# Another division of the first batch, units by quarters of w_out, half-head tile pairs and a load in four parts in a fused attention and feed-forward kernel

## The chip, the core and the metric

The kernel runs on one core of a Trainium2 chip. A core has engines that run side by side, each with its own in-order list of instructions: TensorE (PE, matrix products; its weight loads are shown as PEld), VectorE (DVE), ScalarE (ACT), GpSimd (POOL) and SyncE (SP), which here issues nearly all DMA transfers. They wait for each other through semaphores. Matrix products land in PSUM, a small memory that VectorE and ScalarE read; everything else lies in SBUF. The metric is device time in microseconds (us); lower is better.

## What is computed

A linear attention with cosine weights, then a feed-forward layer on its output:

```python
def phi(x, c, s):
    r = np.maximum(x, 0.0)
    return np.concatenate([r * c, r * s], axis=-1)
q_p = phi(q, cos_w, sin_w)          # q, k, v: 8 batches, 8 heads, 576 rows, 64 wide
k_p = phi(k, cos_w, sin_w)
kv = np.einsum('bhsf,bhsd->bhfd', k_p, v)
z = np.sum(k_p, axis=2)
num = np.einsum('bhsf,bhfd->bhsd', q_p, kv)
den = np.einsum('bhsf,bhf->bhs', q_p, z)[..., None] + 1e-06
x = (num / den)                     # then transposed to 4608 rows of 512
h = x @ w_in                        # 512 x 2048
g = np.maximum(0.01 * h, h)
out = g @ w_out                     # 2048 x 512
```

cos_w and sin_w depend on the row alone.

## The kernel before

**Tiling.** Rows are worked in nine groups of 512: for each of the eight batches its first 512 rows (four tiles of 128, `J = 4`), and a ninth group of the 64 rows left over in each batch. All products take 16-bit operands. A group goes through these steps:

- loads of q, k and v (`load_main`, and `load_kvtail` for the 64 leftover rows) into float32 buffers of the pool `stage` (seven of them, shared with the weights);
- `q_prep`, `k_main` and `k_tail` make relu(x)·cos and relu(x)·sin in 16 bits; the arithmetic of all three is in the helper `phi_half` (L220 when ScalarE does it, L222 on another engine). `v_main` and `v_tail` cast v (helper `copy`, L228 on ScalarE, L230 elsewhere);
- the prepared q is transposed, on TensorE (`q_transpose`, L329, with a copy out of PSUM into `qpT`) for the first two batches and by DMA (L310) after that;
- `kv_mm` (L260, L270) forms k·v with its column of ones for z, four heads at a time; the result is copied to `kv` (L291 for a half of the heads, L282 for all);
- `num` (L339) or, for a pair of tiles on half the heads, `num_half` (L374) multiplies qpT with kv; `divide` (L350, L354, L355, all on VectorE) makes the quotient;
- the quotient is transposed into xT: `x_transpose_half` (L391, copy L395), `x_transpose` (L403) or a DMA (L321);
- `ffn1` (L417) is product one, in 16 column tiles m of w_in, each of four chunks of depth; ScalarE applies the leaky relu to two tiles at once (L425);
- `ffn2` (L440) is product two, in units (tile, quarter): a quarter is four of the 16 depth tiles and needs one of four loads of w_out. After the fourth quarter of a tile the result is copied (`ffn2_out`) and written out (L454).

**Order.** The order of the instructions on every engine is the order in which the program writes them. For the first two batches (numbered 0 and 1 in the code) it is written out by hand; from then on `weave` puts steps (`at(position, step)`) between units of products one and two by their positions. An engine that waits holds up everything behind it in its list.

**PSUM.** There are three pools of buffers: `h` and `o` with two buffers each, `n` with one. A step that takes a buffer waits until the previous user's reader is done.

**Loads.** All loads are issued by SyncE and share one hardware queue; at most eight transfers are tracked at a time, so the ninth is issued when the first has landed. The order at the start is: q in two halves of the heads, the tails of k and v, k and v in halves of the heads, w_in in eight pieces (`load_w1`, L138; cast by POOL in `cast_w1`), two quarters of w_out (`load_w2`, L142; cast by VectorE in `cast_w2`), q of batch 1 and its tails, the other two quarters, k and v of batch 1 in halves, and then q, k and v of batch 2 (the third batch).

**Dummy products.** `idle(n)` (L162) puts n products of zeros into TensorE's list where it would otherwise stand still.

**The stretch that the change touches.** For batch 0 VectorE prepares all of q, the k tail, the v tail and most of k; ScalarE copies the four qpT, casts half of v and does two pieces of k. Product one of batch 0 begins on half-width tiles as soon as a pair of row tiles is ready. In batch 1's part, the units of product two of batch 0 run in this order, with four q transposes of batch 1 between them:

```python
order = [(0, 0), (1, 0), (2, 0), (3, 0), (0, 1), (1, 1), (2, 1), (3, 1), (2, 2), (3, 2)]
```

and the rest of its units lie between the k·v products and numerators of batch 1.

Of the kernel before, what the change touches and what calls it, by code (L numbers as in the profile page):

```python
# [9 lines left out]
dt = mybir.dt  # L10
# [8 lines left out]
def kernel(  # L19
# [61 lines left out]
    def load_main(nm, src, b, parts=(0, 1)):  # L81

        if parts[0] == 0:
            st[nm, b] = stage.tile([P, H, J, D], dt.float32, name=f"{nm}st", tag="stage")
        lo, hi = 4 * parts[0], 4 * parts[-1] + 4
        nc.sync.dma_start(  # L86
            st[nm, b][:, lo:hi],
            src[b, lo:hi, 0:MAIN, :].rearrange("h (p j) d -> p h j d", j=J),
        )
# [26 lines left out]
    def load_halves(b):  # L116
# [5 lines left out]
    w1 = [  # L122
        [const.tile([P, 2, 512], dt.float16, name=f"w1_{i}_{cp}") for cp in range(2)]
        for i in range(DFF // 512)
    ]
# [7 lines left out]
    def load_w1(i, cp):  # L133

        if cp == 0:
            st["w1", i] = stage.tile([P, NKC, 512], dt.float32, name="w1st", tag="stage")
        sl = slice(2 * cp, 2 * cp + 2)
        nc.sync.dma_start(st["w1", i][:, sl], w1v[:, sl, 512 * i : 512 * (i + 1)])  # L138
# [11 lines left out]
    for i in range(NB):  # L150
        for cp in range(2):
            load_w1(i, cp)
# [73 lines left out]
    def copy(eng, o, i):  # L226
        if eng is ACT:
            nc.scalar.copy(o, i)  # L228
        else:
            eng.tensor_copy(o, i)  # L230
# [69 lines left out]
    def q_prep(g, j, lo=0, hi=H):  # L300
        src, c, _ = q_src(g, j)
        if lo == 0:
            st["qp", g, j] = qppool.tile([P, H, F], dt.float16, name="qp", tag="qp")
        qp = st["qp", g, j]
        phi_half(DVE, qp[:, lo:hi, 0:D], src[:, lo:hi], cos_t[:, c : c + 1])
        phi_half(DVE, qp[:, lo:hi, D:F], src[:, lo:hi], sin_t[:, c : c + 1])
# [59 lines left out]
    def num_half(g, jp, hg, where):  # L366

        if hg == 0:
            st["xp", g, jp] = qppool.tile([P, 2, H, D], dt.float16, name="xp", tag="qp")
        ps = psum(where, [P, 2, 512], dt.float32, "ps_numh")  # L370
        for o in range(2):
            for hh in range(4):
                h = 4 * hg + hh
                nc.tensor.matmul(  # L374
                    ps[:, o, hh * NE : (hh + 1) * NE],
                    lhsT=st["qpT", g, 2 * jp + o][:, h, :],
                    rhs=kv[g][:, h, :],
                )
        divide(ps, st["xp", g, jp][:, :, 4 * hg : 4 * hg + 4, :])

    def x_transpose_half(g, jp, hg, ps=None, out=True):

        if ("xT", g) not in st:
            st["xT", g] = xtpool.tile([P, NKC, MAIN], dt.float16, name="xT")
        xp = st["xp", g, jp]
        if ps is None:
            ps = psum("o", [P, 2, 2 * P], dt.float16, "ps_xth")
        for cc in range(2):
            for o in range(2):
                h = 4 * hg + 2 * cc  # L390
                nc.tensor.transpose(  # L391
                    ps[:, cc, o * P : (o + 1) * P], xp[:, o, h : h + 2, :], ident
                )
        if out:
            nc.scalar.copy(  # L395
                st["xT", g][:, 2 * hg : 2 * hg + 2, jp * 2 * P : (jp + 1) * 2 * P], ps
            )
# [10 lines left out]
    def ffn1(g, m, lo=0, hi=MAIN, chunks=range(NKC), where="h"):  # L408
# [7 lines left out]
        for c in chunks:  # L416
            nc.tensor.matmul(  # L417
                ps[:, m % 2, lo:hi],
                lhsT=w1[m // 4][c // 2][:, c % 2, m % 4 : 512 : 4],
                rhs=xT[:, c, lo:hi],  # L420
                start=(c == 0 and lo == 0),
                stop=(c == NKC - 1 and hi == MAIN),
            )
# [61 lines left out]
    def cast_w1(i, cp, eng):  # L485
        sl = slice(2 * cp, 2 * cp + 2)
        copy(eng, w1[i][cp], st["w1", i][:, sl])

    def cast_w2(i, eng):
        copy(eng, w2[:, 4 * i : 4 * i + 4, :], st["w2", i])  # L490
# [3 lines left out]
    for hg in range(2):  # L494
        for j in range(2):
            q_prep(0, j, 4 * hg, 4 * hg + 4)
    for j in range(J):
        if j > 1:
            q_prep(0, j)
        q_transpose(0, j, ACT)  # L500
        idle(1)
    kp_tiles(0)
    k_tail(0, DVE, DVE)
    v_tail(0, DVE)
    for j in range(J):
        k_main(0, j, DVE, DVE, 0, 4)
    v_main(0, 0, 4, ACT)
    for j in range(2):
        k_main(0, j, ACT, DVE, 4, 8)
    idle(6)  # L510
    kv_half(0, 0, "o")
    for j in range(2, J):
        k_main(0, j, DVE, DVE, 4, 8)
    v_main(0, 4, 6, DVE)
    v_main(0, 6, 8, ACT)
    idle(1)
    num_half(0, 0, 0, "n")
    num_half(0, 1, 0, "h")
    idle(3)
    kv_half(0, 1, "o")  # L520
    for i in range(NB):
        for cp in range(2):
            cast_w1(i, cp, POOL)
    x_transpose_half(0, 0, 0)
    num_half(0, 0, 1, "n")
    half = 2 * P
    for m in range(2):
        ffn1(0, m, 0, half, range(0, 2))
    x_transpose_half(0, 1, 0)
    for m in range(2, 4):  # L530
        ffn1(0, m, 0, half, range(0, 2))
    num_half(0, 1, 1, "n")
    x_transpose_half(0, 0, 1)
    for m in range(4):
        ffn1(0, m, half, MAIN, range(0, 2))
# [14 lines left out]
    load_main("q", q, 2)  # L550
# [37 lines left out]
    cast_w2(3, DVE)  # L588
# [4 lines left out]
    for j in range(J):  # L593
        at(5 + j, q_transpose, 1, j, ACT, "h")
        at(9, k_main, 1, j, ACT, DVE, 0, 4)
    at(9, v_main, 1, 0, 2, DVE)
    at(9, v_main, 1, 2, 4, ACT)
    order = [(0, 0), (1, 0), (2, 0), (3, 0), (0, 1), (1, 1), (2, 1), (3, 1), (2, 2), (3, 2)]
    weave([(n, f2(0, 4 * tt + part)) for n, (tt, part) in enumerate(order)], steps)
    for tt in (2, 3):  # L600
        ffn2(0, 4 * tt + 3, None)
    ffn2_out(0, 2, DVE)
    ffn2_out(0, 3, DVE)
    ffn2(0, 2)
    kv_half(1, 0, "h", False)
    k_main(1, 0, ACT, DVE, 4, 8)
    kv_half_out(1, 0)
    for j in range(1, J):
        k_main(1, j, ACT if j < 3 else DVE, DVE, 4, 8)
    v_main(1, 4, 6, POOL)  # L610
    v_main(1, 6, 8, ACT)
    ffn2(0, 4 + 2)
    num_half(1, 0, 0, "h")
    num_half(1, 1, 0, "n")
    ffn2(0, 3, None)
    kv_half(1, 1, "h")
    ffn2_out(0, 0, ACT)
    ffn2_mm(0, 1, 12, 14)
    num_half(1, 0, 1, "h")
    num_half(1, 1, 1, "h")  # L620
    ps = psum("n", [P, 2, MAIN], dt.float16, "ps_x")
    for jp in range(2):
        x_transpose_half(1, jp, 0, ps[:, :, jp * 2 * P : (jp + 1) * 2 * P], False)
    nc.scalar.copy(st["xT", 1][:, 0:2, :], ps)  # L624
    ffn2_mm(0, 1, 14, 16)
    ffn2_out(0, 1, DVE)
    ps = psum("o", [P, 2, 2, 2 * P], dt.float16, "ps_x1")
    x_transpose_half(1, 0, 1, ps[:, 0])
    for m in range(2):
        ffn1(1, m, 0, MAIN, range(0, 2))  # L630
    x_transpose_half(1, 1, 1, ps[:, 1])
    for m in range(2, 4):
        ffn1(1, m, 0, MAIN, range(0, 2))
    for m in range(4):
        ffn1(1, m, 0, MAIN, range(2, 4))
# [4 lines left out]
    for m in range(4, NFT):  # L640
        units.append((8 + m / 2, f1(1, m, "n" if m < 6 else "h")))
# [39 lines left out]
    kv_steps(2, 9.7, 0.5, 13, DVE, 2)  # L681
    for j in range(J):
        at(13.5 + 1.1 * j, num, 2, j)
        at(14.8 + 1.1 * j, x_transpose, 2, j, "o" if j < 2 else "h")
# [53 lines left out]
```

## Time and profile before

| | |
|---|---|
| median of 3 runs | 295.77 us (295.47 to 295.80) |
| profiled execution | 296.48 us |
| its span, first to last instruction | 294.7 us |
| TensorE clock granted over the span | 1.00 |
| HBM read, written | 36.70 MB, 9.44 MB |
| product one (L417) | 592 matmuls, 142.6 us busy |
| product two (L440) | 560 matmuls, 139.5 us busy |
| dummy products (L162) | 28 |

The span and everything in the profile come from one execution, whose time is 0.7 us above the median. In the lists of groups and in the timeline an instruction is named by line, engine, operation and what it writes and reads; `x8` is a count; in brackets stands how long the engine had been idle and who released it. A matmul's recorded length overlaps that of the next, so the distance of starts, and not the length, tells how long one holds TensorE. Busy shares in tenths over 40 slices of 7.4 us show where the engines work:

```
PE   7799999999999999999999999999999999999995
DVE  6951488945846816823562356233323211000011
ACT  4846366754352722642263226322222232222200
DMA  7999999999999999989683997416671211011132
```

The DMA engines are busy without a break for the first 17 slices (to about 125 us), most densely to 60 us.

### The profile page before, as it was taken

What the parts mean: (1) busy time and instruction counts of PE and PEld (TensorE: products, weight loads), DVE (VectorE), ACT (ScalarE), POOL (GpSimd) and SP (SyncE); (2) the same over time, 40 slices, a digit from 0 to 9 for tenths busy, and PEclk for the clock granted to TensorE, in tenths of its full rate; (3) what the DMA queues carried; (4) which work ended last, traced back from release to release, by engine and by line L of the source; (5) the groups of instructions that cost most, each with busy time, mean ns of one, the idle gap of its engine ahead of it and who ended that gap; (6) DMA issues with size and microseconds to landing.
All of it is one profiled execution on the core that took longest, in us unless ns stands there. A gap on an engine that the chain in (4) does not pass through costs nothing.

```text
span 294.7 us, 4802 instructions
## 1 busy us (share of the span) xinstructions
PE 286.4 (97%) x1932; PEld 153.9 (52%) x1932; DVE 129.9 (44%) x329; ACT 117.9 (40%) x143; POOL 11.0 (4%) x20
## 2 busy tenths in 40 slices
PE   7799999999999999999999999999999999999995
PEld 3585556565465455555545554555445544444444
DVE  6951488945846816823562356233323211000011
ACT  4846366754352722642263226322222232222200
POOL 2064000000000000000000000000000000000000
PEclk9999999999999999999999999999999999999999
DMA  7999999999999999989683997416671211011132
GB/s 222 361 385 406 325 362 331 300 155 336 232 271 325 179 265 335 178 158 332 171 152 82 292 276 148 107 55 145 145 160 51 73 53 38 36 46 60 39 71 71
DMA packets 88773, 56.93 MB, mean 193 GB/s; under 512 B 56880, under 2 KB 81712, under 8 KB 88240
## 3 DMA queue, kind: packets, MB, share of 16 engines
q1 hardware_dynamic: 88672, 56.57, 74.2%
q8 instruction: 15, 0.25, 0.4%
q14 instruction: 6, 0.05, 0.1%
q10 hardware_dynamic: 80, 0.07, 0.1%
HBM read 36.70 MB, written 9.44 MB: 157 GB/s over the span
## 4 chain that ended last, share of the span: by engine, by line
PE 81%; DMA 8%; SPq 6%; ACT 1%; issue 1%; DVE 1%; ACTq 0%
PE ps_h L417 38%; PE ps_o L440 37%; SPq L96 4%; DMA w2st<-in_moe_w_out_dram 4%; DMA w1st<-in_moe_w_in_dram 4%; PE ps_num L339 3%; PE ps_kv L270 2%; SPq L86 1%; DMA out_dram<-osb 1%; SPq L138 1%; ACT vmain L228 1%; SPq L142 1%; PE ps_kv L260 1%; DVE w L230 0%; PE ps_numh L374 0%
## 5 line engine op out<-in xcount | busy, mean ns | idle before, releaser
L417 PE MATMUL ps_h<-xT,w 128*128 128x512 f16 (+1 forms) x592 | 142.6, 373 | 0.3 <-ACT xT L624 0.2
L440 PE MATMUL ps_o<-w,g 128*128 128x512 f16 x560 | 139.5, 379 | 0.3 <-DVE w L230 0.3
L425 ACT ACTIVATE g<-ps_h 128x1024 f16<-128x1024 f32 x72 | 73.5, 1024 | 132.9 <-PE ps_h L417 132.7
L417 PEld LDWEIGHTS <-w 128*128 128x128 f16 x592 | 64.4, 113 | 52.3 <-issue 0.3
L440 PEld LDWEIGHTS <-g 128*128 128x128 f16 x560 | 54.1, 98 | 62.0 <-issue 0.6
L230 DVE COPY osb<-ps_o 128x512 f32<-128x512 f32 x34 | 23.4, 690 | 80.1 <-PE ps_o L440 80.1
L350 DVE TENSOR_SCALAR den<-ps_num 128x8 f32<-128x8 f32 x28 | 4.6, 166 | 52.9 <-PE ps_num L339 52.9
L355 DVE TENSOR_TENSOR xs<-ps_num,rden 128x512 f16<-128x512 f32 x28 | 19.4, 691 | 1.0
L222 DVE TENSOR_SCALAR qp<-qst,cos_t 128x512 f16<-128x512 f32 (+1 forms) x34 | 15.8, 465 | 4.9 <-DMA qst<-in_q_dram 4.9
L222 DVE TENSOR_SCALAR kpm<-kst,sin_t 128x512 f16<-128x512 f32 (+1 forms) x40 | 16.5, 428 | 0.8 <-DMA kst<-in_k_dram 0.8
L222 DVE TENSOR_SCALAR qp<-qst,sin_t 128x512 f16<-128x512 f32 (+1 forms) x34 | 15.8, 465 | 0.0
L339 PEld LDWEIGHTS <-qpT 128*128 128x128 f16 (+1 forms) x256 | 11.2, 101 | 7.3 <-issue 1.7
L222 DVE TENSOR_SCALAR kpm<-kst,cos_t 128x512 f16<-128x512 f32 (+1 forms) x29 | 13.0, 449 | 0.1
L228 ACT CAST vmain<-vst 128x1024 f16<-128x1024 f32 (+1 forms) x14 | 12.9, 953 | 0.4 <-DMA vst<-in_v_dram 0.3
L339 PE MATMUL ps_num<-kv,qpT 128*128 128x66 f16 (+1 forms) x256 | 12.4, 194 | 0.0
L270 PEld LDWEIGHTS <-kpm 128*128 128x128 f16 x256 | 10.5, 97 | 2.6 <-DVE kpm L222 0.7
L228 ACT COPY qpT<-ps_qt 128x1024 f16<-128x1024 f16 x8 | 7.8, 1019 | 7.0 <-PE ps_qt L329 7.0
L162 PE MATMUL ps_idle<-blank 128*128 128x512 f16 x28 | 9.1, 462 | 1.2 <-DVE blank L157 1.2
L230 DVE CAST w<-w2st 128x2048 f16<-128x2048 f32 x4 | 4.9, 1228 | 10.7 <-DMA w2st<-in_moe_w_out_dram 10.7
L230 POOL CAST w<-w1st 128x1024 f16<-128x1024 f32 x8 | 8.3, 1042 | 15.1 <-DMA w1st<-in_moe_w_in_dram 15.0
L270 PE MATMUL ps_kv<-vmain,kpm 128*128 128x66 f16 x192 | 8.1, 193 | 0.0
L354 DVE RECIPROCAL rden<-den 128x8 f32<-128x8 f32 x36 | 7.3, 203 | 1.2
(57 smaller groups left out, 97.1 us busy)
## 6 DMA issues: line engine op xcount, KB each, us to landing
out_dram<-osb SPq DMA_DIRECT2D x32, 256.0 KB, 2.5
qst<-in_q_dram SPq DMA_DIRECT2D x7, 1024.0 KB, 6.5
kst<-in_k_dram SPq DMA_DIRECT2D x6, 1024.0 KB, 8.8
vst<-in_v_dram SPq DMA_DIRECT2D x6, 1024.0 KB, 8.9
w1st<-in_moe_w_in_dram SPq DMA_DIRECT2D x8, 512.0 KB, 11.0
w2st<-in_moe_w_out_dram SPq DMA_DIRECT2D x4, 1024.0 KB, 11.5
kst<-in_k_dram SPq DMA_DIRECT2D x4, 512.0 KB, 8.7
vst<-in_v_dram SPq DMA_DIRECT2D x4, 512.0 KB, 8.7
```

Of the source, the lines that this page charges most:

```text
L96: nc.sync.dma_start(t[o * TAIL : (o + 1) * TAIL], v4[o])
L162: nc.tensor.matmul(ps, lhsT=blank[:, 0:P], rhs=blank)
L222: eng.tensor_scalar(out=o, in0=i, scalar1=0.0, scalar2=col, op0=ALU.max, op1=ALU.mult)
L228: nc.scalar.copy(o, i)
L230: eng.tensor_copy(o, i)
L270: nc.tensor.matmul(ps[:, (2 * cc + o) * NE : (2 * cc + o + 1) * NE], lhsT=kpm[:, h, j, :], rhs=vmain[b % 2][:, h, j, :], start=False, stop ...
L339: nc.tensor.matmul(ps[lo:hi, h // 4, (h % 4) * NE : (h % 4 + 1) * NE], lhsT=qpT[:, h, lo:hi], rhs=kv[b][:, h, :],)
L354: nc.vector.reciprocal(rden, den)
L355: nc.vector.tensor_tensor(out=xs, in0=ps[:, :, 0 : 4 * NE].rearrange("p a (b e) -> p a b e", e=NE)[:, :, :, 0:D], in1=rden.rearrange("p (a ...
L417: nc.tensor.matmul(ps[:, m % 2, lo:hi], lhsT=w1[m // 4][c // 2][:, c % 2, m % 4 : 512 : 4], rhs=xT[:, c, lo:hi], start=(c == 0 and lo == 0 ...
L425: nc.scalar.activation(st["g", g][:, m - 1 : m + 1, :], ps, AF.Lrelu)
L440: nc.tensor.matmul(st["ps_o", g, tt], lhsT=st["g", g][:, m, tt * P : (tt + 1) * P], rhs=w2[:, m, :], start=(m == 0), stop=(m == NFT - 1),)
```

## The change

What it does:

- Batch 0: ScalarE prepares the fourth tile of q and takes the cos half of k more often; POOL casts the v tail and a quarter of v; VectorE copies one of the four qpT. The transposes of q and the dummy products (32 instead of 28) stand in another order. The first piece of w_in is loaded and cast in two. Both numerators of the second half of the heads are formed one behind the other, in different PSUM buffers.
- Product two of batch 0: the units run quarter by quarter over all four tiles, up to the third quarter; two more units stand ahead of the first k·v product of batch 1, and none are left after the second. The q transposes of batch 1 stand one unit later. The cast of the last quarter of w_out is in two halves.
- Batch 1: the transposes of the first half of the heads go through two `o` buffers and two copies, instead of one `n` buffer and one copy; ScalarE copies out two of the four results of product two instead of one. Product one of batch 1 takes its first six column tiles in two halves of the depth, instead of four tiles.
- Batch 2: q is loaded in four loads by partitions (56, 40, 24, 8). Its k·v product, numerators and transposes stand one position later.

```diff
+    def load_main(nm, src, b, parts=(0, 1), span=(0, P)):
...
-            st[nm, b][:, lo:hi],
-            src[b, lo:hi, 0:MAIN, :].rearrange("h (p j) d -> p h j d", j=J),
+            st[nm, b][p0:p1, lo:hi],
+            src[b, lo:hi, J * p0 : J * p1, :].rearrange("h (p j) d -> p h j d", j=J),
...
-    for i in range(NB):
-        for cp in range(2):
-            load_w1(i, cp)
+    w1_parts = [(0, 0, 1), (0, 1, 1), (0, 2, 2)]
+    for i in range(1, NB):
+        w1_parts += [(i, 0, 2), (i, 2, 2)]
+    for part in w1_parts:
+        load_w1(*part)
...
+    def x_transpose_half_out(g, jp, hg):
+        nc.scalar.copy(
+            st["xT", g][:, 2 * hg : 2 * hg + 2, jp * 2 * P : (jp + 1) * 2 * P],
+            st["xth", g, jp, hg],
+        )
...
     for hg in range(2):
-        for j in range(2):
-            q_prep(0, j, 4 * hg, 4 * hg + 4)
+        for j in range(J):
+            q_prep(0, j, 4 * hg, 4 * hg + 4, ACT if j == 3 else DVE)
+    kp_tiles(0)
+    q_transpose(0, 0, ACT)
+    idle(1)
+    q_transpose(0, 1, ACT)
+    idle(1)
+    k_tail(0, DVE, DVE)
+    v_tail(0, POOL)
+    k_main(0, 0, ACT, DVE, 0, 4)
+    for j in range(1, J):
+        k_main(0, j, DVE, DVE, 0, 4)
+    q_transpose(0, 2, ACT, "n")
+    idle(1)
+    v_main(0, 0, 2, DVE)
+    v_main(0, 2, 4, ACT)
+    q_transpose(0, 3, DVE)
+    idle(9)
+    kv_half(0, 0, "o")
     for j in range(J):
-        if j > 1:
-            q_prep(0, j)
-        q_transpose(0, j, ACT)
-        idle(1)
-    kp_tiles(0)
-    k_tail(0, DVE, DVE)
-    v_tail(0, DVE)
-    for j in range(J):
-        k_main(0, j, DVE, DVE, 0, 4)
-    v_main(0, 0, 4, ACT)
-    for j in range(2):
         k_main(0, j, ACT, DVE, 4, 8)
+    num_half(0, 0, 0, "h")
+    num_half(0, 1, 0, "n")
+    v_main(0, 4, 6, ACT)
+    v_main(0, 6, 8, POOL)
     idle(6)
-    kv_half(0, 0, "o")
-    for j in range(2, J):
-        k_main(0, j, DVE, DVE, 4, 8)
-    v_main(0, 4, 6, DVE)
-    v_main(0, 6, 8, ACT)
-    idle(1)
-    num_half(0, 0, 0, "n")
-    num_half(0, 1, 0, "h")
-    idle(3)
+    x_transpose_half(0, 0, 0)
     kv_half(0, 1, "o")
...
+    ps = psum("h", [P, 2, 512], dt.float32, "ps_numh")
     for m in range(2):
-        ffn1(0, m, 0, half, range(0, 2))
-    x_transpose_half(0, 1, 0)
+        ffn1(0, m, 0, half, range(0, 1))
+    num_half(0, 0, 1, None, ps)
+    num_half(0, 1, 1, "n")
+    for m in range(2):
+        ffn1(0, m, 0, half, range(1, 2))
+    for m in range(2):
+        ffn1(0, m, half, MAIN, range(0, 2))
+    x_transpose_half(0, 0, 1)
...
-    load_main("q", q, 2)
+    for p0, p1 in ((0, 56), (56, 96), (96, 120), (120, P)):
+        load_main("q", q, 2, span=(p0, p1))
...
-    cast_w2(3, DVE)
+    cast_w2(3, DVE, 0, 2)
+    cast_w2(3, DVE, 2, 4)
...
-        at(5 + j, q_transpose, 1, j, ACT, "h")
-        at(9, k_main, 1, j, ACT, DVE, 0, 4)
-    at(9, v_main, 1, 0, 2, DVE)
-    at(9, v_main, 1, 2, 4, ACT)
-    order = [(0, 0), (1, 0), (2, 0), (3, 0), (0, 1), (1, 1), (2, 1), (3, 1), (2, 2), (3, 2)]
+        at(6 + j, q_transpose, 1, j, ACT, "h")
+    order = [(tt, part) for part in range(3) for tt in range(J)]
...
     for tt in (2, 3):
         ffn2(0, 4 * tt + 3, None)
     ffn2_out(0, 2, DVE)
     ffn2_out(0, 3, DVE)
-    ffn2(0, 2)
     kv_half(1, 0, "h", False)
     k_main(1, 0, ACT, DVE, 4, 8)
     kv_half_out(1, 0)
+    ffn2(0, 3, None)
...
-    ffn2(0, 4 + 2)
+    ffn2_out(0, 0, ACT)
     num_half(1, 0, 0, "h")
     num_half(1, 1, 0, "n")
-    ffn2(0, 3, None)
+    ffn2(0, 7, None)
     kv_half(1, 1, "h")
-    ffn2_out(0, 0, ACT)
-    ffn2_mm(0, 1, 12, 14)
+    ffn2_out(0, 1, ACT)
+    x_transpose_half(1, 0, 0)
+    x_transpose_half(1, 1, 0)
     num_half(1, 0, 1, "h")
-    num_half(1, 1, 1, "h")
-    ps = psum("n", [P, 2, MAIN], dt.float16, "ps_x")
-    for jp in range(2):
-        x_transpose_half(1, jp, 0, ps[:, :, jp * 2 * P : (jp + 1) * 2 * P], False)
-    nc.scalar.copy(st["xT", 1][:, 0:2, :], ps)
-    ffn2_mm(0, 1, 14, 16)
-    ffn2_out(0, 1, DVE)
-    ps = psum("o", [P, 2, 2, 2 * P], dt.float16, "ps_x1")
-    x_transpose_half(1, 0, 1, ps[:, 0])
+    num_half(1, 1, 1, "n")
     for m in range(2):
         ffn1(1, m, 0, MAIN, range(0, 2))
-    x_transpose_half(1, 1, 1, ps[:, 1])
+    x_transpose_half(1, 0, 1)
     for m in range(2, 4):
         ffn1(1, m, 0, MAIN, range(0, 2))
-    for m in range(4):
+    x_transpose_half(1, 1, 1)
+    for m in range(4, 6):
+        ffn1(1, m, 0, MAIN, range(0, 2), "n")
+    for m in range(6):
         ffn1(1, m, 0, MAIN, range(2, 4))
...
-    for m in range(4, NFT):
-        units.append((8 + m / 2, f1(1, m, "n" if m < 6 else "h")))
+    for m in range(6, NFT):
+        units.append((8 + m / 2, f1(1, m)))
...
-    kv_steps(2, 9.7, 0.5, 13, DVE, 2)
+    kv_steps(2, 9.7, 0.5, 14, DVE, 2)
     for j in range(J):
-        at(13.5 + 1.1 * j, num, 2, j)
-        at(14.8 + 1.1 * j, x_transpose, 2, j, "o" if j < 2 else "h")
+        at(14.5 + 1.1 * j, num, 2, j)
+        at(15.8 + 1.1 * j, x_transpose, 2, j, "o" if j < 2 else "h")
```

## Prediction

> **What bounds the kernel now.** I read the page's busy shares first, then TensorE's waits, then the timeline of the first 62 us, then the issues and landings of the loads.
>
> ```profile
> span 294.7 us, 4802 instructions
> ...
> PE 286.4 (97%) x1932; PEld 153.9 (52%) x1932; DVE 129.9 (44%) x329; ACT 117.9 (40%) x143; POOL 11.0 (4%) x20
> ```
>
> TensorE is the bound; what can be won is its idle time. The list of its waits (total us, times, longest) is short:
>
> ```profile
> PE ps_numh L374 <- ACT kv L291: 1.1, 2, 0.9
> ...
> PE ps_o L440 <- DVE w L230: 0.3, 1, 0.3
> ...
> PE ps_h L417 <- ACT xT L624: 0.2, 1, 0.2
> ```
>
> Warm matmuls of 512 columns start 0.216 us apart (the 52 of the last stretch of the chain take 11.24), transposes 0.056, 66-column ones 0.032, 256-column ones 0.109. Against these pitches TensorE is gap-free from 53 us on, but for 0.6 us at 102 us, in code that the diff does not touch. So the change can act in two places: the front, and 40 to 53 us. The front (start, length, engine; in brackets the idle time before):
>
> ```profile
> 15.91 0.38 ACT L291 CAST kv<-ps_kvh 128x264 f16<-128x264 f32 x1 [1.15 <-PE ps_kvh L270]
> ...
> 16.80 0.17 DVE L350 TENSOR_SCALAR den<-ps_numh 128x8 f32<-128x8 f32 x1
> ...
> 17.98 0.43 PE L374 MATMUL ps_numh<-kv,qpT 128*128 128x66 f16 x8
> ...
> 18.45 0.17 DVE L350 TENSOR_SCALAR den<-ps_numh 128x8 f32<-128x8 f32 x1 [0.52 <-PE ps_numh L374]
> ...
> 19.64 0.40 PE L391 MATMUL ps_xth<-ident,xp 128*128 128x128 f16 x4
> ...
> 19.87 12.27 PE L417 MATMUL ps_h<-xT,w 128*128 128x256 f16 x64
> ```
>
> The second numerator (17.98) waits until the first's division has freed the one "n" buffer; its division starts 0.52 us idle; the last transposes start at 19.64. From there TensorE runs without a gap until 42.4. Then:
>
> ```profile
> 39.00 1.23 DVE L230 CAST w<-w2st 128x2048 f16<-128x2048 f32 x1 [0.78 <-DMA w2st<-in_moe_w_out_dram]
> ...
> 40.67 1.89 PE L440 MATMUL ps_o<-w,g 128*128 128x512 f16 x8
> ...
> 42.90 2.75 PE L440 MATMUL ps_o<-w,g 128*128 128x512 f16 x12 [0.34 <-DVE w L230]
> ...
> 47.67 0.62 POOL L230 CAST vmain<-vst 128x512 f16<-128x512 f32 x1 [21.40 <-DMA vst<-in_v_dram]
> ...
> 49.54 0.59 ACT L228 COPY osb<-ps_o 128x512 f32<-128x512 f32 x1
> ...
> 51.91 1.02 PE L417 MATMUL ps_h<-xT,w 128*128 128x512 f16 x4 [0.18 <-ACT xT L624]
> ```
>
> The third quarter of w_out lands just before 39.00 and is ready at 40.23; TensorE takes it up at 40.67, only 0.44 later. The fourth makes TensorE wait at 42.40 (40.67 + 8 x 0.216) until 42.90. Three more gaps follow by the pitches: 0.20 (before 49.69), 0.25 (before 51.33), 0.34 (before 51.91). Together 1.29 us.
>
> **The change, part by part.**
>
> *First batch.* VectorE keeps 12 of 16 q halves: starts 0.263 apart (rows 4.63, 4.90, 5.17), six from 4.63, six from 6.22, done 7.80 (before: 8.80). The k tail takes two, to 8.33. k's first half lands at 8.87 (issue 4.57 + 4.3); seven pieces to 10.7, v's piece 0.42 to 11.1. ScalarE has four q pieces (0.41 each, pace of L220) from 4.97, done 7.0, before the first qpT copy (7.3, unchanged). The first product k.v starts at 11.15 instead of 12.02, its copy at 11.95 instead of 13.53 (ScalarE is free), the first two numerators at 12.35 instead of 13.94. VectorE's copy of qpT 3 out of PSUM is not in this trace: at least 0.69 (128x512 out of PSUM, row L355), at most twice that; it ends at 12.5 at the latest, before k's second half lands (12.65), so it costs nothing.
> VectorE then does four k pieces and no v: free at 13.71 instead of 14.57. Divisions (1.04 apart, 1.13 long) end at 14.83 and 15.86. ScalarE, though, now does four k pieces from 12.71 and v (0.62): ready 14.97, so the second k.v product starts at 15.11 (before 15.09), its copy ends at 16.32 (before 16.29). Nothing won to here. The two numerators now have a buffer each: 16.42 and 16.68, divisions back to back from 16.87, end 18.0 and 19.03, last transposes 19.15. Front gain 19.64 - 19.15 = 0.49 us. The first w1 piece, halved, lands at about 14.8 (half of 1.36 before 15.5) and is cast by 15.5: hidden.
>
> *Units by quarters.* Product two now starts at 31.98 - 0.49 = 31.49. Eight units (4 x 0.216 = 0.865) and three transposes of q (8 x 0.056 = 0.445; the fourth has moved behind the ninth unit) bring TensorE to the third quarter at 31.49 + 6.92 + 1.34 = 39.75. It is ready at 40.23 + 0.05 whatever TensorE does, since no load ahead of it changes in bytes or order. TensorE waits 0.53: the front's gain is gone here. From 40.28 there are no waits: six units, one transposed q, k.v, numerators and two more units until the second k.v at 40.28 + 8 x 0.865 + 0.445 + 0.63 + 0.51 = 48.79. The fourth quarter (first half cast by 42.25) is needed at 44.2: its 0.50 stall is gone. k.v ends at 49.42, where before it ended at 49.2 with 4 matmuls (0.86) still to do.
>
> *Pairs on half the heads.* Now ScalarE's order counts: kv copy 49.61, osb copy 49.89 to 50.48 (0.28 behind it, as 49.26 and 49.54 before). The second transposes need the "o" buffer that this osb copy frees: 50.53, a new wait of 0.9. Then numerators, xT copy 50.96 to 51.55, and product one of batch 2 at 51.60 instead of 51.91. Its first 24 matmuls with two transposes end at 51.60 + 5.19 + 0.45 = 57.24; before 51.91 + 5.19 + 0.22 = 57.32. Sum so far: -0.08 us.
>
> *POOL beside VectorE.* In the changed order VectorE's k pieces run from 46.75 to 48.1, so the 0.62 us cast of v on POOL (47.67) falls on them; before they ended at 47.56. What that does is shown once:
>
> ```profile
> 1.69 0.62 DVE L205 CAST vmain<-ones 128x64 f16<-128x64 f32 x1
> 1.72 1.06 POOL L208 MEMSET vtail<- 128x528 f16 x2
> ...
> 3.00 0.20 DVE L205 CAST vmain<-ones 128x64 f16<-128x64 f32 x1
> ```
>
> The same cast takes 0.62 beside a POOL memset and 0.20 without. If VectorE is held until POOL ends (48.29), its last k piece frees it at 48.57 instead of 48.05, the divisions end at 50.74 and the second transposes start at 50.80 instead of 50.53: +0.27. Bounds: 0 and +0.4; I take +0.27, by the row. [...] The POOL cast of the v tail at 7.1 can hold VectorE by some 0.6 likewise; 0.5 of it falls into the wait for k at 8.3 to 8.87.
>
> *q in four loads, k.v of batch 3 one position later.* q, k and v of that batch land at 50.7, 53.8 and 57.4 (issue plus time to landing). VectorE prepares them from 53.3 on, about 61.2 done; k.v now comes after 24 more matmuls, at 62.45 (before: 60.77, with VectorE done at 60.82). Cover 1.2 us, cost nothing. Four more dummy matmuls lie in waits.
>
> Sum: -0.49 (front) + 0.53 (third quarter) - 0.50 (fourth) - 0.79 (three old gaps) + 0.89 (second transposes) + 0.34 (wait for xT, 51.26 to 51.60) + 0.27 (POOL) = +0.25 us; by the end times above -0.08 + 0.27 = +0.19. The 0.06 between them is rounding in the pitches; I take +0.2. The profiled run took 296.48 (span 294.7, 1.8 around it); the median is 295.77. On the median: 295.95 us.
>
> **Rivals.**
> *The gain gets through (faster).* If the third quarter lands 0.5 us earlier, its wait is gone and, with POOL the one that waits, the sum is -0.6: 295.2. For it: all loads run in one backlogged queue (w_out's quarters land 10.1 to 13.4 us after issue), and small shifts add up. Against: nothing ahead of it is smaller. Chance 0.18.
> *The third quarter later (slower).* Each 0.1 us later costs 0.1 in the new order; before, 0.44 were free. Landing at 39.5 instead of 39.0 gives +0.7: 296.5. It decides as soon as the landing slips. Against: the three runs lie within 0.33 us. Chance 0.15.
> *q's four loads delay k and v (slower).* If 56, 40, 24 and 8 partitions use fewer DMA engines, at half the rate q takes 6 us instead of 3, v lands at 60.4, VectorE needs 2.7 more (58.10 to 60.82 before): 63.1 against 62.45, +0.65 and so 296.6. It decides from a landing of v after 59.75. The trace has no load of such a shape. Chance 0.1. [...]
> *It does not do what it says*: the front is not faster. Up to 0.5 us of that costs nothing either, since the third quarter waits anyway; this belongs to the forecast.
>
> **Numbers.** Forecast, gains and new waits cancel, 295.95: 0.52, own range 295.4 to 296.4. Faster rival 0.18, the two slower ones 0.25, unnamed 0.05 (shared). Range for 8 in 10: 295.0 to 296.8, from the faster case to just past the slower ones. Faster by over 0.2% (0.6 us, what a measurement can tell): 0.2; within: 0.52; slower: 0.28.
>
> **What would show it.** Last front transposes near 19.15; a TensorE wait on VectorE's w cast of some 0.5 us near 39.75 and none at 42; a wait on ScalarE's osb or VectorE's xp of 0.9 to 1.2 near 49.7; product one of batch 2 at 51.6 to 51.9; a k piece beside POOL stretched near 47.7; no wait at k.v of batch 3. It is wrong if the third quarter lands elsewhere than near 39.0, or if a gap opens after 57 us.

## The result, and the profile after

| | before | changed kernel |
|---|---|---|
| median, runs side by side (6 each) | 295.78 us (295.47 to 296.32) | 298.64 us (297.48 to 300.37) |
| a second set | 295.69 us (17 runs) | 298.13 us (296.78 to 299.60, 6 runs) |
| ratio, first set | | 1.0105, 95% interval 1.007 to 1.014 |
| ratio, second set | | 1.0084, 95% interval 1.0053 to 1.0115 |
| span of the profiled execution | 294.7 us | 297.2 us, in the second set 295.5 us |

The changed kernel is about 1% slower; 295.95 us had been predicted. It also varies: its twelve runs lie over 3.6 us, the 23 of before over 1 us (in the later sets before, too, has single runs up to 298.6). So two profiled executions of it are read here, the first of 298.95 us and one from the second set of 297.32 us. The first one's page, with the row of the clock granted to TensorE in tenths over 40 slices:

```profile
span 297.2 us, 4829 instructions
...
PE 287.9 (97%) x1936; PEld 154.8 (52%) x1936; DVE 128.5 (43%) x325; ACT 120.0 (40%) x151; POOL 12.7 (4%) x24
...
PEclk9979999999999999999999999999999999999999
```

TensorE is still the bound, and the clock is not full in the third slice (14.9 to 22.3 us). From its list of TensorE's waits (total us, times, longest), where before had kv, w and xT:

```profile
PE ps_kvh L277 <- DVE vmain L237: 1.4, 1, 1.4
PE ps_xth L398 <- DVE xp L362: 1.2, 3, 0.6
...
PE ps_numh L382 <- ACT kv L298: 0.5, 1, 0.5
...
PE ps_h L429 <- ACT xT L406: 0.2, 1, 0.2
```

No wait on w (the quarters of w_out) is left, neither the new one that was predicted for the third nor the old one for the fourth. In the same execution's timeline (start, length, engine, and in brackets the idle time before):

```profile
10.49 0.35 DVE L229 TENSOR_SCALAR kpm<-kst,sin_t 128x256 f16<-128x256 f32 x1 [1.66 <-DMA kst<-in_k_dram]
...
12.80 0.41 PE L277 MATMUL ps_kvh<-vmain,kpm 128*128 128x66 f16 x8 [1.38 <-DVE vmain L237]
...
14.50 2.56 PE L169 MATMUL ps_idle<-blank 128*128 128x512 f16 x6
...
21.65 0.39 PE L398 MATMUL ps_xth<-ident,xp 128*128 128x128 f16 x4
...
52.79 0.40 PE L398 MATMUL ps_xth<-ident,xp 128*128 128x128 f16 x4 [0.64 <-DVE xp L362]
...
53.86 0.81 PE L429 MATMUL ps_h<-xT,w 128*128 128x512 f16 x3 [0.16 <-ACT xT L406]
```

Here k's first half came 1.6 us late (work on it at 10.49, 8.87 predicted), the six dummy products took 2.56 us because the clock had halved (0.50 from 14.70 to 18.12 us; the second execution shows them with 1.46), the front's last transposes began at 21.65 instead of 19.64, and product one of the second batch at 53.86 instead of 51.91. In the second profiled execution none of that is there, and the front is the predicted one to 0.04 us: work on k at 8.86, the first k·v at 11.13, its copy at 11.95, numerators at 12.38, the second k·v at 15.09, the last transposes at 19.11. VectorE begins the cast of w_out's third quarter at 38.01, TensorE comes to that quarter at 39.69 and does not wait there. The loss comes later:

```profile
38.01 1.23 DVE L237 CAST w<-w2st 128x2048 f16<-128x2048 f32 x1 [0.70 <-DMA w2st<-in_moe_w_out_dram]
...
39.69 1.03 PE L452 MATMUL ps_o<-w,g 128*128 128x512 f16 x4
...
60.66 1.29 DVE L237 CAST vmain<-vst 128x1024 f16<-128x1024 f32 x2 [0.46 <-DMA vst<-in_v_dram]
61.87 0.60 DVE L237 CAST vtail<-vtl 64x256 f16<-64x256 f32 x2
62.50 0.49 DVE L229 TENSOR_SCALAR kpm<-kst,cos_t 128x512 f16<-128x512 f32 x1
...
62.90 0.48 DVE L229 TENSOR_SCALAR kpm<-kst,sin_t 128x512 f16<-128x512 f32 x1
...
63.44 0.33 PE L277 MATMUL ps_kv<-vmain,kpm 128*128 128x66 f16 x5 [0.59 <-DVE kpm L229]
```

v of the third batch has only landed at 60.6 us (57.38 in before). VectorE waits for it, does the last pieces of k behind it, and TensorE stands in the middle of the third batch's k·v. Why v is late shows in the traffic of the DMA engines. The windows of the first profiled execution (stretch, its length, busy time of PE, PEld, DVE, ACT and POOL, clock, busy share of the DMA engines, GB/s; the share adds up the times of packets, which overlap, so it can pass 1):

```profile
42.00:46.00 4.00, 4.00 (x32) 2.23 (x29) 2.05 (x6) 3.35 (x7) 0.00 (x0) 1.00 1.11 301
46.00:50.00 4.00, 4.00 (x49) 2.42 (x48) 1.94 (x5) 2.65 (x8) 0.61 (x1) 1.00 1.12 199
50.00:54.00 4.00, 2.95 (x48) 2.12 (x46) 3.05 (x12) 2.80 (x6) 0.00 (x0) 1.00 1.11 161
```

and the same of the kernel before:

```profile
42.00:46.00 4.00, 3.66 (x30) 1.85 (x29) 3.36 (x8) 2.21 (x5) 0.00 (x0) 1.00 1.10 348
46.00:50.00 4.00, 3.96 (x63) 2.59 (x60) 3.50 (x12) 2.85 (x7) 0.62 (x1) 1.00 1.10 347
50.00:54.00 4.00, 3.73 (x39) 2.27 (x36) 3.72 (x10) 2.22 (x4) 0.00 (x0) 1.00 1.12 303
```

From 46 us on the DMA engines are as busy (1.11 and 1.12, before 1.10 and 1.12) and move little more than half. The second execution has 297, 211 and 214 GB/s in the same stretches. A packet of 1 KB takes 52 ns on average in before between 46 and 50 us, 92 and 87 ns in the two executions of the changed kernel.

### The profile page after: what moved, and what is told of

It is laid out like the page before. It is cut to its first block, busy times and chain, and to the rows that moved or that the text cites. A ratio compares the mean times of both kernels' runs of the same rounds, so it can differ in the third digit from the quotient of the medians.

```text
span 297.2 us, 4829 instructions
## 1 busy us (share of the span) xinstructions
PE 287.9 (97%) x1936; PEld 154.8 (52%) x1936; DVE 128.5 (43%) x325; ACT 120.0 (40%) x151; POOL 12.7 (4%) x24
## 4 chain that ended last, share of the span: by engine, by line
PE 90%; DVE 3%; DMA 3%; ACT 1%; SPq 1%; issue 1%; ACTq 0%
PE ps_h L429 42%; PE ps_o L452 39%; PE ps_num L346 3%; PE ps_kv L277 2%; DMA kst<-in_k_dram 2%; DVE kpm L229 1%; SPq L97 1%; PE ps_idle L169 1%; DMA out_dram<-osb 1%; PE ps_xth L398 1%; DVE xp L362 1%; ACT vmain L235 1%; DVE osb L237 1%; PE ps_qt L336 1%; PE ps_kv L267 1%
## 5 line engine op out<-in xcount | busy, mean ns | idle before, releaser
L237 DVE COPY osb<-ps_o 128x512 f32<-128x512 f32 x33 | 22.7, 691 | 81.0 <-PE ps_o L452 79.6
L362 DVE TENSOR_TENSOR xs<-ps_num,rden 128x512 f16<-128x512 f32 x28 | 19.4, 691 | 1.0
L229 DVE TENSOR_SCALAR kpm<-kst,cos_t 128x512 f16<-128x512 f32 (+1 forms) x26 | 11.9, 458 | 0.0
L169 PE MATMUL ps_idle<-blank 128*128 128x512 f16 x32 | 10.6, 480 | 1.2 <-DVE blank L164 1.2
L235 ACT COPY qpT<-ps_qt 128x1024 f16<-128x1024 f16 x7 | 7.0, 1010 | 5.8 <-PE ps_qt L336 5.8
L237 DVE CAST w<-w2st 128x2048 f16<-128x2048 f32 (+1 forms) x5 | 5.0, 1013 | 9.1 <-DMA w2st<-in_moe_w_out_dram 9.1
L237 POOL CAST w<-w1st 128x1024 f16<-128x1024 f32 (+1 forms) x9 | 8.5, 946 | 2.6 <-DMA w1st<-in_moe_w_in_dram 2.6
```

Source lines behind the costliest of these rows:

```text
L169: nc.tensor.matmul(ps, lhsT=blank[:, 0:P], rhs=blank)
L229: eng.tensor_scalar(out=o, in0=i, scalar1=0.0, scalar2=col, op0=ALU.max, op1=ALU.mult)
L362: nc.vector.tensor_tensor(out=xs, in0=ps[:, :, 0 : 4 * NE].rearrange("p a (b e) -> p a b e", e=NE)[:, :, :, 0:D], in1=rden.rearrange("p (a ...
```

## The experiments

Twelve runs were made, each beside the kernel before on the same chip. "Span" is that of the profiled execution.

| kernel | median us | ratio to before, 95% interval | span |
|---|---|---|---|
| front alone | 295.91 | 1.0008 (0.9999 to 1.0017) | 293.4 |
| q in four loads alone | 297.67 | 1.0062 (1.0044 to 1.0080) | 296.0 |
| middle alone | 297.07 | 1.0044 (1.0032 to 1.0056) | 295.1 |
| changed kernel again | 298.13 | 1.0084 (1.0053 to 1.0115) | 295.5 |
| q in four loads of 32 rows | 297.69 | 1.0067 (1.0043 to 1.0091) | 296.0 |
| q in four loads by heads | 295.81 | 0.9997 (0.9987 to 1.0008) | 294.1 |
| q in four loads of every fourth row | 296.16 | 1.0008 (0.9990 to 1.0026) | 294.0 |
| changed kernel, q in one load | 296.29 | 1.0016 (1.0005 to 1.0026) | 294.8 |
| the same, less on VectorE | 296.06 | 1.0007 (0.9996 to 1.0018) | 293.7 |
| before, fourth batch's k·v later | 295.98 | 1.0007 (0.9994 to 1.0019) | 293.8 |
| less on VectorE, fourth batch's k·v later | 296.02 | 1.0013 (1.0000 to 1.0025) | 293.6 |
| before, fifth batch's k·v later | 295.16 | 0.9981 (0.9968 to 0.9995) | 293.3 |

### One part at a time

From the first profile the front looked guilty, with 2 us lost by 22 us. So the three parts of the diff were put into the kernel before one at a time (theory 1 blames the front, theory 2 q's loads, theory 3 the middle), and the changed kernel was run once more. The front is everything of the diff up to the end of batch 0's product one; the middle everything from the cast of w_out's last quarter to `units`; q's part is

```diff
-    load_main("q", q, 2)
+    for p0, p1 in ((0, 56), (56, 96), (96, 120), (120, P)):
+        load_main("q", q, 2, span=(p0, p1))
...
-    kv_steps(2, 9.7, 0.5, 13, DVE, 2)
+    kv_steps(2, 9.7, 0.5, 14, DVE, 2)
...
-        at(13.5 + 1.1 * j, num, 2, j)
-        at(14.8 + 1.1 * j, x_transpose, 2, j, "o" if j < 2 else "h")
+        at(14.5 + 1.1 * j, num, 2, j)
+        at(15.8 + 1.1 * j, x_transpose, 2, j, "o" if j < 2 else "h")
```

> The kernel before with the change's front alone (batch 0's division among the engines, the two first pieces of w_in apart, three pairs of half tiles); middle and q's load as before. Theory 1 (the front costs it: k's first half and the clock): 297.5 to 298.5 us, that is +1.7 to +2.7, with the granted clock under 1 between 14 and 19 us in some executions and product one of the second batch some 2 us later than before's 51.91. Theory 2 (q's four loads delay k and v of the third batch and cost it): 295.3 to 296.0. Theory 3 (the middle: new order of product two's quarters, copies on ACT): 295.3 to 296.0, as predicted for the front alone (-0.49).

> The kernel before with the third batch's q in four loads, and its k.v with what follows one step later, alone. Theory 1 (front): 295.5 to 296.0, k and v landing up to 5 us later than before's 53.84 and 57.38 but within the cover. Theory 2 (q's loads): 297 to 299, with waits of TensorE between 60 and 75 us, or with large differences from run to run. Theory 3 (middle): as theory 1.

> The kernel before with the middle alone (third and fourth quarter of w_out cast as needed, product two in the order of quarters, the transposes of half tiles apart with their copies on ACT, six units of product one in the second batch's first half). Theory 1 (front): 295.7 to 296.3, from the waits between 45 and 54 us (+0.25 by the two profiled executions). Theory 2 (q's loads): the same. Theory 3 (middle): 297.5 or more.

> The changed kernel once more, for a second trace and for how far its runs spread. Theory 1 (front): a median of 298.6 with runs from 297.4 to 300.4; the late landing of k's first half (10.46 us) and the half clock from 14.7 to 18.1 us need not both be there again, but the second batch's product one begins 1 to 4 us after before's 51.91. Theory 2 (q's loads): product one of the second batch begins within 0.5 us of the first trace's 53.86 and the time varies behind 54 us. Theory 3: the waits between 45 and 54 us vary.

Theory 1 fell: the front alone costs nothing that can be told (295.91, ratio 1.0008). q's part alone costs 2.0 us and varies by 2.2 us from run to run, and the middle alone costs 1.4. The late k and the halved clock of the first profile were one execution's misfortune, and came before q's loads were even issued (from 39.0 us on): a clock mean of 0.994, which 3.4 us at half speed make, was seen in two of the changed kernel's twelve runs and in none of 11 with the front alone, and three of the 93 runs of before beside these experiments have 0.994 or 0.992. The other ten runs of the changed kernel have at least 0.999 and still lie between 296.78 and 300.37 us. No theory was right throughout: 297.07 for the middle lies between the ranges given for it, and the repeated kernel began product one of the second batch at 51.67 us, where theories 1 and 2 had it at 52.9 or later.

With q's part alone, TensorE's first wait comes from a load that was issued *ahead of* q: the second half of the second batch's v lands at 48.7 us, 4.7 us after the first half (46.4 with the front alone, 3.0 after the first half). Both casts and TensorE wait for it:

```profile
48.71 0.62 ACT L229 CAST vmain<-vst 128x512 f16<-128x512 f32 x1 [1.24 <-DMA vst<-in_v_dram]
48.74 0.61 POOL L231 CAST vmain<-vst 128x512 f16<-128x512 f32 x1 [22.58 <-DMA vst<-in_v_dram]
49.40 0.73 PE L271 MATMUL ps_kvh<-vmain,kpm 128*128 128x66 f16 x8 [1.10 <-DVE xp L356]
```

The list names VectorE's xp as releaser of the 1.10 us, but that had ended at 49.36 beside the two casts (49.33 and 49.35). It does not need that xp: with the front alone the same product starts at 47.25 and the xp at 47.75. v set the time. Product two's stretch up to product one of the second batch grows from 19.4 us (front alone) to 21.5. k of the third batch lands at 57.7 instead of 52.6.

With the middle alone, two places show:

```profile
49.57 0.59 ACT L228 COPY osb<-ps_o 128x512 f32<-128x512 f32 x1
49.80 0.69 DVE L355 TENSOR_TENSOR xp<-ps_numh,rden 128x512 f16<-128x512 f32 x1
...
50.54 0.40 PE L390 MATMUL ps_xth<-ident,xp 128*128 128x128 f16 x4 [0.64 <-DVE xp L355]
...
61.36 0.33 PE L270 MATMUL ps_kv<-vmain,kpm 128*128 128x66 f16 x5 [0.35 <-DVE kpm L222]
```

The second transposes wait, as predicted, but for VectorE's second division (ends 50.49) and not for ScalarE's copy (50.16). And the third batch's k·v, which here stands at its old position while six tiles of product one have moved ahead of the positions' count, comes too early by 0.5 us. In this respect the run overstates what the middle costs in the changed kernel, where that product stands one position later.

### What makes the four loads slow

Three theories: the number of loads (A), the unequal shares of the DMA engines (B), or the few partitions that each load writes (C). Two kernels differ from before in q's loads (and the one position) alone. The first takes equal quarters of the rows:

```diff
+    for p0, p1 in ((0, 32), (32, 64), (64, 96), (96, P)):
+        load_main("q", q, 2, span=(p0, p1))
```

The second takes all rows, two heads a time:

```diff
+    for h0 in range(0, H, 2):
+        nc.sync.dma_start(
+            st["q", 2][:, h0 : h0 + 2],
+            q[2, h0 : h0 + 2, 0:MAIN, :].rearrange("h (p j) d -> p h j d", j=J),
+        )
```

> The kernel before with the third batch's q in four loads of 32 rows each (0-31, 32-63, 64-95, 96-127) in place of 56, 40, 24 and 8, and the one step later; nothing else of the change. Theory A (four issues and four places among the loads in flight cost it): 297.7 us as with 56, 40, 24, 8; k of the third batch lands near 57.7. Theory B (the shares of the 16 DMA engines are unequal, 11 rows on some and none on others): 295.5 to 296.0, k near 52.7 and v of the second batch near 46.4, with 350 GB/s between 46 and 54 us. Theory C (each load writes few partitions at a time, and packets to those take longer): 297 us or more, under 280 GB/s between 46 and 54 us, 1 KB packets at 75 ns or more in place of 51.

> The kernel before with the third batch's q in four loads of two heads each over all 128 partitions, and the one step later; nothing else of the change. Theory A (number of loads): 297.7 us, k of the third batch near 57.7. Theory B (unequal shares) and theory C (few partitions at a time) both: 295.5 to 296.0, k near 52.7, 350 GB/s between 46 and 54 us.

Both came out as theory C has it: 297.69 us by rows, 295.81 by heads. Equal loads did not help the time, and four loads as such did not hurt. The semaphores of the change's four loads rise once at issue and then 14, 10, 12 and 8 times as data land; those of 32 rows rise 16 times, as those of whole loads do. That each rise is the share of one DMA engine was the author's reading; no run here shows it. With the unequal loads k of the third batch lands later, at 57.7 us against 55.9 with 32 rows each, but both kernels take 297.7 us. A third kernel kept the 32 rows of a load but spread them, to tell rows that lie side by side from the number of rows in a load:

```diff
+    for r in range(4):
+        nc.sync.dma_start(
+            st["q", 2][r:P:4],
+            q[2, :, 0:MAIN, :].rearrange("h (p j) d -> p h j d", j=J)[r:P:4],
+        )
```

> The kernel before with the third batch's q in four loads of 32 rows each, but rows 0, 4, 8 and so on in the first, 1, 5, 9 in the second, and the one step later; nothing else of the change. [...] If 32 rows in a load, or two rows for each engine, are what is slow: 1.25 us apart as those of rows 0-31 and so on were, k near 56, 297.7 us.

It is as quick as by heads, within the noise. The four loads of 256 KB land at 48.89, 50.14, 51.40 and 52.63 us with rows side by side, 1.25 us apart (209 GB/s), and at 47.62, 48.37, 49.12 and 49.88 with rows spread, 0.75 us apart (350 GB/s). The windows with rows side by side:

```profile
44.00:46.00 2.00, 2.00 (x28) 1.27 (x27) 1.94 (x6) 0.94 (x4) 0.00 (x0) 1.00 1.15 203
46.00:48.00 2.00, 1.52 (x22) 0.92 (x21) 1.86 (x8) 0.95 (x3) 0.23 (x1) 1.00 1.12 210
48.00:50.00 2.00, 1.53 (x26) 1.03 (x26) 0.58 (x1) 1.00 (x3) 0.38 (x1) 1.00 1.13 213
```

and with rows spread:

```profile
44.00:46.00 2.00, 2.00 (x26) 1.26 (x25) 2.00 (x6) 1.20 (x4) 0.00 (x0) 1.00 1.10 346
46.00:48.00 2.00, 2.00 (x31) 1.29 (x30) 1.93 (x8) 1.50 (x4) 0.62 (x1) 1.00 1.11 350
48.00:50.00 2.00, 1.96 (x43) 1.56 (x40) 1.41 (x6) 0.87 (x2) 0.00 (x0) 1.00 1.10 347
```

The drop begins at 44 us, while loads issued before q are still in flight: they are slowed too (the second half of the second batch's v lands at 47.7 us, 46.9 with rows spread). Few partitions in a load are not slow by themselves: with 32 spread ones the engines move 346 to 350 GB/s between 44 and 50 us, with 32 side by side 203 to 213. Whether this lies with the partitions written or with the addresses read is not shown: spreading the rows spreads the addresses in DRAM as well, and no run here changes one without the other. The spread of runs is still wider with spread rows (2.0 us) than by heads (0.8), but before varied by 3.3 us beside it in that set.

### The changed kernel with q in one load, and with less on VectorE

The first of these is the changed kernel with `load_main("q", q, 2)` for the four loads, the later position kept. The second also has

```diff
     ffn2_out(0, 2, DVE)
-    ffn2_out(0, 3, DVE)
     kv_half(1, 0, "h", False)
     k_main(1, 0, ACT, DVE, 4, 8)
     kv_half_out(1, 0)
+    ffn2_out(0, 3, ACT)
...
-    v_main(1, 6, 8, ACT)
+    v_main(1, 6, 8, POOL)
```

> The changed kernel with the third batch's q in one load again; the one step later stays. If the slow load is what makes the changed kernel vary and wait near 62 us: 296.3 to 296.9 us with runs within 1 us of one another (before 295.7, front +0.0 to +0.2, middle +0.5 behind the copies and +0.24 in the first 32 matrix products of the second batch's product one), no wait near 61 to 63 us, v of the second batch at 46.4 and k of the third at 52.7. If the middle or the front makes it vary: runs 2 us or more apart, and 298 us.

> The same with one copy of product two's result (quarter of tokens 3) moved from DVE to ACT and the last cast of the second batch's v from ACT to POOL. If DVE's queue between 45.8 and 51 us (two copies of 0.65, then the pieces of k, then two divisions) is what makes the half tiles' transposes late: the wait of 0.80 ahead of the second transposes shrinks by 0.3 to 0.65 us, and the time by as much: 295.8 to 296.4. If the copies on ACT are the cause, as the prediction has it: no better than the run with q in one load, or worse by up to 0.5 us.

With q in one load the changed kernel takes 296.29 us, 2.1 less than the mean of its two medians, its runs lie within 0.7 us, and there is no wait in the third batch's k·v. So the partial loads account for nearly all of the loss and for the spread. What is left is 0.6 us (0.05 to 0.26%). Taking 0.65 us of copy from VectorE's queue (and a cast from ScalarE's) gave 0.2 us, but the intervals of the two overlap, so that gain is not shown. Its trace:

```profile
46.59 1.41 POOL L237 CAST vmain<-vst 128x512 f16<-128x512 f32 x2 [20.28 <-DMA vst<-in_v_dram]
46.84 0.70 DVE L229 TENSOR_SCALAR kpm<-kst,sin_t 128x256 f16<-128x256 f32 x1
...
48.63 0.40 PE L398 MATMUL ps_xth<-ident,xp 128*128 128x128 f16 x4
...
49.66 0.40 PE L398 MATMUL ps_xth<-ident,xp 128*128 128x128 f16 x4 [0.64 <-DVE xp L362]
```

The wait that was to shrink (0.80 by the pitch, ahead of the second transposes) did not: two divisions follow each other by 1.03 to 1.04 us in both runs (xp at 47.88 and 48.91 here, at 48.95 and 49.99 without the two moves), and nothing stands between the transposes. The wait ahead of the first transposes shrank instead, from 0.56 to 0.17. The time from product two's start to product one of the second batch went from 20.2 to 19.6 us; with before's middle and the new front it is 19.4.

### A version that beats both

Every kernel so far has TensorE waiting 0.57 us near 102 us. In the kernel before:

```profile
103.03 0.22 PE L260 MATMUL ps_kv<-vtail,kpt 128*128 128x132 f16 x1 [0.41 <-ACT vtail L228]
```

It was taken for the fourth batch's k·v, and that was moved in two kernels:

```diff
-    kv_steps(3, 20, 0.7, 24, ACT)
-    out_steps(3, 24.5, 1.4, 1)
+    kv_steps(3, 20, 0.7, 24.5, ACT)
+    out_steps(3, 25, 1.25, 1)
```

> The kernel before with the fourth batch's k.v half a step (one unit, 0.86 us) later and its numerators from 25 on, 1.25 apart, in place of 24.5 and 1.4. Every kernel so far shows TensorE waiting 0.57 us near 102 us there for ScalarE's cast of v's tail. If the wait is only a matter of place: gone, and 295.0 to 295.3 us. If the numerators or transposes behind it are then late (a wait near 115 to 131 us): 295.7 or more.

> The same half step in the changed kernel with q in one load, one copy on ACT and one cast on POOL: 296.06 less 0.57, that is 295.3 to 295.7 us, if the wait is a matter of place; no better than 296.0 if what follows is late.

Neither moved it: the wait is as long as before (0.41 us on the record) and ends at 102.17 and 102.06 us. The positions count 16 to a batch, and group 1 of the units ends, by the count of product two's matmuls, at 99.0 us, which is position 32: 102 us is position 34, the fifth batch's k·v.

```diff
-    kv_steps(4, 28, 1.2, 34, ACT)
+    kv_steps(4, 28, 1.2, 34.6, ACT)
```

> The kernel before with the fifth batch's k.v two units of TensorE's work (8 matrix products of 512 columns, 1.73 us) later: the wait near 102 us stayed where it was when the fourth batch's k.v was moved, so it is the fifth batch's. If the wait is only a matter of place: gone, nothing late behind it, 295.0 to 295.4 us. If ScalarE's casts or the numerators behind it set it: 295.6 or more, with a new wait between 103 and 112 us.

```profile
101.29 0.83 ACT L228 CAST vtail<-vtl 64x256 f16<-64x256 f32 x2
101.60 1.03 PE L417 MATMUL ps_h<-xT,w 128*128 128x512 f16 x4
...
102.46 1.03 PE L440 MATMUL ps_o<-w,g 128*128 128x512 f16 x4
103.33 0.22 PE L260 MATMUL ps_kv<-vtail,kpt 128*128 128x132 f16 x1
```

Two units now stand where the wait was, ScalarE's cast ends (102.12) before the product is due, and no new wait opens: 295.16 us, ratio 0.9981 (0.9968 to 0.9995). It is the fastest kernel here.

## Why the prediction was wrong

- *First batch, -0.49 us.* Right step by step, too large as a gain. The second profiled execution has every step of it within 0.04 us, and five executions with this front begin product two at 31.0 to 31.6 us (31.49 predicted; the sixth, with the halved clock, at 34.0). But the eight with the old front begin it at 31.4 to 32.0, and the 31.98 that the prediction subtracted from is the latest of them; by the means of the two groups, 31.3 and 31.6, the gain is 0.3. Alone it won nothing measurable, though: its median span is 293.8 us beside 293.9, and 0.3 us more lie outside the span (2.1 around it, 1.8 in before), which no view here explains.
- *Third quarter, +0.53, and fourth quarter, -0.50.* Neither was there. VectorE begins the third quarter's cast at 38.0 us, not 39.0, and TensorE comes to it at 39.69 (39.75 predicted) without a wait. The prediction took the landings of one execution for those of the kernel; in the twelve other executions that cast begins at 37.6 to 38.5 us, old front or new. In before's execution 15 of the load's 16 semaphore increments had come by 37.69 us and the last at 38.98, so the last came 1.3 us behind the others; with the front alone the last two came at 37.63 and 37.75. And the old stall of 0.50 at the fourth quarter is 0 to 0.26 in the seven of the twelve that have the old order of units. The two terms cancel, so the sum did not suffer; that was luck. The condition of the faster rival, a third quarter 0.5 us earlier, held, but its gain of 0.6 did not come: it counts the 0.50 as won, most of which the kernel before does not lose, and takes POOL for the engine that waits, which it was not near 47 us, where it is VectorE's piece of k that went from 0.35 to 0.70 us.
- *Second transposes +0.89, wait for xT +0.34, old gaps -0.79.* Size right, with the next term: by the pitches 0.41 + 0.80 + 0.33 us in the first profile and 0.46 + 0.81 + 0.32 in the second, where 0.89 + 0.34 + 0.27 had been forecast. The first of the three stands ahead of the first transposes. The cause was half wrong. With the middle alone ScalarE's copy ends 0.3 us before VectorE's division, which comes last.
- *POOL beside VectorE, +0.27.* Right as a delay of VectorE near 47 us, not shown as one of TensorE: a piece of k takes 0.70 us beside POOL's cast and 0.35 without, in each of the four executions in which the two meet; POOL's cast is stretched less, to 0.67 to 0.80 us from 0.61. But in the first profile the two do not meet, and the waits above add up to 1.54 us there, to 1.59 in the second, where they do. It can also go the other way: near 7.2 us, in the run with less on VectorE, POOL's first cast of the v tail took 1.43 us (0.39 to 0.55 in the other five executions with this front) and VectorE's pieces beside it kept their 0.34.
- *Product one of the second batch at 51.60 to 51.9.* 51.67 in the second profiled execution, 51.81 with q in one load.
- *q in four loads, cost nothing, cover 1.2 us.* This is the step that failed. The DMA engines move 160 to 215 GB/s instead of 300 to 350, v of the third batch lands at 60.6 to 62.1 instead of 57.4, and the cover is gone: 0.76 us of wait by the pitches in the second profile. The third rival had just this (half the rate, v at 60.4, +0.65), and was given 0.10; its price was too low as well, since q's part alone costs 2.0 us and the changed kernel loses 2.1 by it. Two things were wrong in weighing it. Only the later loads were thought to be delayed, whereas the last half of the second batch's v, issued ahead of q, lands 4.0 to 4.7 us after the first half instead of 3.0 and has no cover at all in some executions. And the rival puts the loss down to fewer DMA engines; four loads of 32 rows, whose semaphores rise 16 times like those of a whole load, were as slow (297.69 us against 297.67).
- Without that step the forecast holds: 296.29 us with q in one load, 295.95 predicted, inside its own range of 295.4 to 296.4. In part this is luck. An estimate with the terms as the runs show them (-0.3 for the front, 0 and -0.1 for the quarters, +0.75 for the middle) gives +0.3 us; the ratio of that run stands for +0.15 to +0.77.
- What is not settled: which wait each of the slower, unprofiled runs had. The profiled ones show several (1.4 us ahead of the first k·v and the halved clock, 1.3 at the second batch's v, 0.8 at the third batch's k·v), and one with rows side by side had 1.3 us at a numerator near 117 us.

## What to carry to other kernels

When a load is split, split it along the free dimension or take every fourth partition, as in the two splits that cost nothing that can be told here (295.81 and 296.16 us): loads of neighbouring partitions took 297.67 and 297.69 us, and in the changed kernel they brought the traffic of everything in flight from 347 to 199 GB/s between 46 and 50 us, also that of a load issued before them. The cover of a delayed load has to be counted at every consumer whose data is in flight then, not at the load's own consumer alone. And a stall seen in one profiled execution belongs to that execution until a second one shows it: the late third quarter and the stall at the fourth, on which the prediction built two terms, were gone in the next trace.

## What was not expected of the hardware

TensorE's clock halved although it had stood idle for no longer than 1.4 us at a time. In the first profile (stretch, length, TensorE's busy time first, clock and GB/s at the end):

```profile
7.86:11.28 3.42, 3.42 (x32) 2.07 (x30) 1.76 (x7) 2.27 (x4) 0.29 (x1) 1.00 1.04 349
11.28:14.70 3.42, 1.57 (x36) 1.25 (x35) 3.28 (x12) 2.37 (x6) 0.00 (x0) 1.00 1.08 373
14.70:18.12 3.42, 3.42 (x24) 2.03 (x23) 1.86 (x5) 1.94 (x5) 2.25 (x4) 0.50 1.06 388
```

The stretches of full speed are whole multiples of one length in these traces: 10.24 us is 3 times 3.413 and 279.89 us 82 times here, 290.13 us is 85 times 3.413 in before, and the stretch at half speed is one such length. So the clock seems to be set anew every 3.41 us, and the three stretches above lie on that grid. In the middle one TensorE was busy for 1.57 of 3.41 us (46%) by the records, its longest wait 1.4 us, and then it ran at half speed for one stretch. In the other 13 executions the least busy stretch on the grid between 4 and 20 us has 2.14 us (q in four loads of every fourth row; 2.45 in before), and full speed follows. Whether busy time sets the clock, where between 1.57 and 2.14 us a limit would then lie, and whether the kind of product counts, is not shown.
